# Talking-heads attention and squared-ReLU feed-forward: a planner that holds on-chip relayouts when a burst of loads begins

## The chip, the cores and the metric

The kernel runs on one core of one Trainium2 chip. The metric is the device time of one execution in microseconds (us), as the median of several runs. Besides that there is one profiled execution, from which all single durations are taken.

## The reference

Eight batches, twelve heads, 448 positions, head size 64; then a feed-forward block of 768 to 2048 to 768 on the attention's output of 3584 tokens.

```python
scores = scale * np.matmul(q, k.transpose(0, 1, 3, 2))
scores = np.einsum('bhij,hg->bgij', scores, w_pre)      # heads are mixed before the softmax
scores = scores - np.max(scores, axis=-1, keepdims=True)
attn = np.exp(scores)
attn = attn / (np.sum(attn, axis=-1, keepdims=True) + 1e-09)
attn = np.einsum('bhij,hg->bgij', attn, w_post)         # and once more after it
out = np.matmul(attn, v)
x = out.transpose(0, 2, 1, 3).reshape(B * S, H * D)
h = np.maximum(x @ w_in, 0.0)
result = h * h @ w_out
```

## The kernel before

**The work and its pieces.** A batch is cut into 45 *chunks* of up to ten query rows times twelve heads, 120 partitions. The head mixing is then a matmul over a chunk's 120 rows. The steps, with the lines of the profile:

- `score` (L681): scores of one head pair and one row block, evacuated by DVE (L487) or ACT (L489) into `snat`, where rows are positions. `b` is the batch, `r` the row block 0 to 3.
- `relayout` / `move` (L709): DMAs on SP's queue that gather a chunk's rows out of `snat` into `sch`, where rows are (position, head). There are two `snat` buffers, so a score block's evacuation overwrites the block before last and must see that block's relayouts landed.
- `chunk`: the mixing matmul (L807; in batch 0 partly L813, straight from the queries through weights prepared on DVE at L796), row minimum on DVE (L818, scores carry a minus sign), exponential with sum on ACT (L821), reciprocal on DVE (L827), the second mixing's weights times that on POOL (`wq`, L830), second mixing and transpose in one (L837), evacuation into `atb` (L487, L489).
- `av` (L882): times the values, evacuated into `xt`.
- `unit`: the feed-forward for 128 or 256 tokens: L941, ReLU on DVE (L955) or ACT (L959), square on POOL (`h`, L962), L980, evacuation into `osb`, and stores (L1004).
- `x_piece` (from batch 2 on): K and Q of the next batch, copied into `kn` and `qn` on POOL or DVE (L612), then transposed by DMA on SP's queue (L625, L631); `x_tail` (L596) does the same for the tail rows. In batches 0 and 1 PE transposes (L549, L577).
- Loads of q, k, v and the feed-forward weights are DMAs issued by POOL (L352, L358, L363, L1076, L1082). Those of the next batch come in a burst of eight, once a batch.
- Idle matmuls (L1191) stand where the plan has PE idle early in the kernel.
- At the start the mixing weights are made: `near_mix` (L467) on DVE, turned by one matmul (L1054), put by DVE (L1060).

**What sets the order.** A planner. Each step is an operation with one or several possible engines, a cost in ns, a priority, a latency `lat` after it and its dependencies. `Planner.run` plays all engines forward in its own time, each always taking its most urgent ready operation, and records the operations in that order. The recorded order is the program: each engine then works through its own list, and waits where the data is not there. The planner's times set the order and nothing else.

**Transfers in the planner.** Two modelled queues, `LOAD` (POOL's loads) and `DMA` (relayouts and stores). `moved(queue, rows, alone, shared, ...)` is a transfer of so many rows with a cost per row when the other queue is empty or not. A relayout is an SP operation followed by such a transfer; a load likewise from POOL; a store (`st_op`) likewise. If `DMA` is empty while loads run, a relayout first waits for the loads that are ahead (`ahead`, at most `FIFO` rows).

`AHEAD` is by how many chunks the relayout of a chunk is more urgent than its mixing; the scores' priority follows from it too.

Of the kernel before, what the change touches and what calls it, by code (L numbers as in the profile page):

```python
# [39 lines left out]
PIECE = NPAIR // 2  # L40
NE = 6
NSCH = 11
AHEAD = 7.0
FIFO = 50
IDLE_NS, IDLE_COLS, IDLE_FROM, IDLE_END, IDLE_LOW = 112, 256, 1300, 130000, 0.62
SPELL, PHASE, DROP, RISE = 3413, 1700, 0.4, 0.8
ROWS, COLS = 1, 2
TURN = 95
LATER = 2
NEAR_LAST = 2e6  # L50
OSTEP = 2
GS, ONE = [(0, 1, 2)], [(0,), (1,), (2,)]
# [26 lines left out]
NEAR_AT = 5  # L79
# [42 lines left out]
class Planner:  # L122
# [8 lines left out]
    def add(self, eng, ns, pri, fn, deps=(), lat=60, bank=None, frees=None, mode=0):  # L131
        op = Op(eng if isinstance(eng, dict) else {eng: ns}, lat, pri, fn, list(deps), bank, frees, mode)
        self.ops.append(op)
        return op
# [6 lines left out]
    def run(self):  # L141
        order, events, n = [], [], 0
# [21 lines left out]
        t, mode, clock = 0, 0, Clock()  # L164
        queues = {"LOAD": Queue(), "DMA": Queue()}

        def settle():
            nonlocal n
            a, z = queues["LOAD"], queues["DMA"]
            for x, y in ((a, z), (z, a)):  # L170
                if x.op is None:
                    continue
                x.left -= (t - x.at) * x.rate
                x.at = t
                rows, alone, shared = x.op.rows
                x.rate = 1.0 / (alone if y.op is None else shared + y.op.rows[2])
                x.turn += 1
                heapq.heappush(events, (t + max(x.left, 0.0) / x.rate, n, (x, x.turn)))
                n += 1

        while True:
            for eng, heap in ready.items():
                if eng in queues:
                    x = queues[eng]
                    y = queues["LOAD"]
                    if eng == "DMA" and x.op is None and heap and y.op is not None and x.last != t and x.wait < t:
                        ahead = max(0.0, y.left - (t - y.at) * y.rate) + sum(z[2].rows[0] for z in ready["LOAD"])
                        x.wait = t + int(min(ahead, FIFO) * y.op.rows[1])
                        heapq.heappush(events, (x.wait, n, None))
                        n += 1  # L190
                    if eng == "DMA" and x.wait > t:
                        continue
                    while x.op is None and heap:
                        op = heapq.heappop(heap)[2]
                        op.eng, op.at = eng, t
                        order.append((op, []))
                        if op.rows[0] == 0:
                            heapq.heappush(events, (t + op.lat, n, op))
                            n += 1
                            continue  # L200
                        x.op, x.left, x.at, x.rate = op, float(op.rows[0]), t, 0.0
                        settle()
                    continue
                if busy[eng] > t:
                    continue
                kept, short, first = [], False, None
                while heap:
                    item = heapq.heappop(heap)
                    op = item[2]
                    if op.eng is not None:  # L210
                        continue
                    wide = len(op.bank) > 1
                    if not fits(op) or (short and op.bank and op.bank[0][0] in HOLD):
                        short = short or wide
                        kept.append(item)
                        continue
                    if eng == "PE" and mode and op.mode != mode and first is None:
                        first = item
                        kept.append(item)
                        continue  # L220
                    if first is not None:
                        if op.mode != mode or op.pri > first[0] + STAY[mode]:
                            kept.append(item)
                            if op.pri > first[0] + STAY[mode]:
                                op, item = first[2], first
                                kept.remove(first)
                            else:
                                continue
                    args = []
                    break  # L230
                else:
                    item = None
                    if first is not None:
                        kept.remove(first)
                        item, op, args = first, first[2], []
                if item is None and eng == "PE" and free and IDLE_FROM <= t < IDLE_END and (
                    t < 9000 or clock.at(t) > 1 or clock.share(t - SPELL, t) < IDLE_LOW
                ):
                    op = Op({"PE": 0}, 0, 0, self.still, [], None, None, mode)
                    op.eng, op.ns, op.at = "PE", IDLE_NS * clock.at(t), t  # L240
                    clock.spells.append((t, t + op.ns))
                    order.append((op, [free[0], mode]))
                    busy[eng] = t + op.ns
                    heapq.heappush(events, (t + op.ns, n, None))
                    n += 1
                if item is not None:
                    for key in op.bank:
                        held[key] = free.pop(0)
                        room[key[0]] -= 1
                        room["mix"] -= key[0] != "f"  # L250
                        args.append(held[key])
                    if len(op.engs) > 1:
                        args.append(eng)
                    op.eng, op.ns, op.at = eng, op.engs[eng], t
                    if eng == "PE":
                        op.ns = (op.ns + TURN * (op.mode != mode)) * clock.at(t)
                        clock.spells.append((t, t + op.ns))
                        mode = op.mode
                    order.append((op, args))
                    busy[eng] = t + op.ns  # L260
                    heapq.heappush(events, (t + op.ns, n, None))
                    heapq.heappush(events, (t + op.ns + op.lat, n + 1, op))
                    n += 2
                for item in kept:
                    heapq.heappush(heap, item)
            if not events:
                break
            t = events[0][0]
            while events and events[0][0] == t:
                op = heapq.heappop(events)[2]  # L270
                if op is None:
                    continue
                if isinstance(op, tuple) and isinstance(op[0], Queue):
                    x, turn_ = op
                    if x.turn == turn_:
                        done = x.op
# [27 lines left out]
def kernel(  # L304
# [11 lines left out]
    nc = tc.nc  # L316
# [175 lines left out]
    pl = Planner()  # L492
    pl.banks, pl.most = banks, MOST
    add = pl.add
# [32 lines left out]
    h_op, sq_op, o_op, st_op = {}, {}, {}, {}  # L527
# [141 lines left out]
    def score(b, r, group):  # L669
# [13 lines left out]
        first = min(place_of(b, c) for c in range(C0[r], (C0 + [NCHUNK])[r + 1]) if not is_direct(b, c)) - b * NCHUNK  # L683
        pri = b * NCHUNK + first - AHEAD - 0.6 - (0.7 if r == 0 else 1.4) * (NPAIR - p)
        n = b * (NJ + 1) + r - 2
# [20 lines left out]
        return r, c - C0[r]  # L706

    def move(n, pri, ns, deps, outs, srcs, lat):
        op = add("SP", ns, pri, lambda: nc.sync.dma_start(out=outs, in_=srcs), deps, lat=680)  # L709
        rows, alone, shared = (12, 70, 38) if ns > 700 else (6, 70, 38)  # L710
        done = pl.moved("DMA", rows, alone, shared, 0, [op], 500)
        relay.setdefault(n, []).append(done)
        return done

# [209 lines left out]
    def unit(pair, ui):  # L924
        a, z = units_of(pair)[ui]
# [46 lines left out]
        for mt in range(w // 128):  # L972
            whole = not (z == W2B and mt == 1 and pair == B // 2 - 1)
            cuts = [0, 384, DMODEL] if whole else [0, 384, 640, DMODEL]
            for nt, (c0, c1) in enumerate(zip(cuts, cuts[1:])):
# [16 lines left out]
                si = ix_store[0]  # L992
# [6 lines left out]
                if nt == 1 or not whole:  # L999
                    done = []  # L1000
                    for rows, dst, o in pieces(pair, a + mt * 128, None if whole else (c0, c1)):
                        side_ = not whole and rows <= CI
                        def store(dst=dst, o=o, rows=rows, si=si, e0=0 if whole else c0, e1=DMODEL if whole else c1, eng=nc.scalar if side_ else nc.sync):
                            eng.dma_start(out=dst, in_=osb[si % 2][o:o + rows, e0:e1])  # L1004
                        done.append(add("ACT" if side_ else "SP", 510 if rows <= CI else 930, FILL, store, evs))
                    st_op[si] = pl.moved("DMA", 8, 140, 130, 0, done, 1500)
            if whole:
                ix_store[0] += 1

# [53 lines left out]
    backed_far.append(add("POOL", 420, FAR_AT, far_back, [picked]))  # L1063
    fetched = add("DVE", 900, NEAR_AT, pick_near, [walled, k_in[0, 2]])
    masked = add("DVE", 500, NEAR_AT, near_masks, [k_in[0, 2]])
    mixed = add("DVE", 500, NEAR_AT, near_mix, [fetched, masked])
    backed.append(add("POOL", 420, NEAR_AT, near_back, [fetched, masked]))
    w_ready = add(
        "DVE", 300, NEAR_AT, w_put, [add("PE", 200, NEAR_AT, keep(("m", "w"), w_turn), [mixed], lat=200, bank=("m", "w"))], frees=("m", "w"),
# [162 lines left out]
```

## Time and profile before

| | us |
|---|---|
| three runs | 578.25, 578.26, 579.37 |
| median | 578.26 |
| the profiled execution's own time | 577.99 |
| its span, first to last instruction | 576.2 |
| busy PE in it | 565.1 |
| busy DVE, ACT, POOL | 510.2, 445.9, 329.4 |
| mean granted clock of TensorE | 0.999 |

PE is the engine of the matmuls, DVE the vector engine, ACT the scalar engine, POOL the GpSimd engine and SP the engine that issues most DMAs; PEld is the weight load of PE. A line of the timeline or of a group tells engine, line of the kernel, operation, what it writes and reads, and how many; in brackets the engine's idle time before it and who ended that. A matmul's record is longer than its share of PE's time, since matmuls overlap: a run of L807 matmuls starts one each 0.19 us, though each record lasts 0.35 us.

### The profile page before, as it was taken

The page shows a single profiled execution, that of the slowest core. Times are in us where ns is not written, and L with a number is a line of the kernel's source. Part 1 is how long each engine was busy: PE and PEld are TensorE (multiplying, and loading weights), DVE is VectorE, ACT ScalarE, POOL GpSimd, SP SyncE. Part 2 cuts the span into 40 slices and gives each one's busy share as a digit, 9 for nine tenths or more (in the row PEclk, how much of TensorE's full clock was granted, in tenths as well). Part 3 has the DMA queues.
Part 4 walks back from the last instruction along what each step waited for, and adds up shares of the span by engine and source line. Part 5 has one row for each costly group of instructions (what it writes and reads, how often), then busy time and mean ns, then how long its engine had stood idle before and what let it go on. Part 6 is the DMA issues. An engine that isn't in the chain of part 4 may idle for free.

```text
span 576.2 us, 16829 instructions
## 1 busy us (share of the span) xinstructions
PE 565.1 (98%) x5830; PEld 407.5 (71%) x5830; DVE 510.2 (89%) x1124; ACT 445.9 (77%) x1185; POOL 329.4 (57%) x609
## 2 busy tenths in 40 slices
PE   8999999999999999999999999999999999999997
PEld 5668766786776767677667677777758676767784
DVE  7999998999999999989899988999799898989442
ACT  5798988878778887988888988888888888888100
POOL 8267445764575548646567357845767444735341
PEclk9999999999999999999999999999999999999999
DMA  9999849963898639963697638984497646322021
GB/s 135 211 182 224 158 116 208 163 151 87 132 202 156 159 100 184 173 151 111 137 181 148 164 104 144 188 152 139 109 205 158 147 121 117 124 81 75 1 56 55
DMA packets 131678, 80.79 MB, mean 140 GB/s; under 512 B 59286, under 2 KB 126600, under 8 KB 131592
## 3 DMA queue, kind: packets, MB, share of 16 engines
q1 hardware_dynamic: 84760, 56.88, 40.3%
q0 software_dynamic: 46784, 22.81, 30.8%
q8 instruction: 45, 0.74, 0.6%
q14 instruction: 41, 0.34, 0.2%
q10 hardware_dynamic: 48, 0.02, 0.0%
HBM read 45.61 MB, written 11.01 MB: 98 GB/s over the span
## 4 chain that ended last, share of the span: by engine, by line
PE 87%; DVE 6%; DMA 3%; ACT 2%; issue 1%; POOL 0%; DVEq 0%; ACTq 0%; POOLq 0%
PE bank L980 24%; PE bank L941 23%; PE bank L837 12%; PE bank L807 11%; PE bank L882 7%; PE bank L681 6%; DMA sch<-snat 3%; PE bank L813 2%; DVE mn L818 1%; DVE atb L487 1%; DVE snat L487 1%; PE bank L1191 1%; ACT es L821 1%; DVE qn L612 1%; ACT snat L489 0%
## 5 line engine op out<-in xcount | busy, mean ns | idle before, releaser
L821 ACT ACTIVATE es<-bank,mn 120x448 bf16<-120x448 f32 x360 | 228.5, 643 | 37.0 <-DVE mn L818 32.6
L818 DVE TENSOR_REDUCE mn<-bank 120x1 f32<-120x448 f32 x360 | 209.7, 611 | 1.2 <-PE bank L807 1.1
L830 POOL TENSOR_SCALAR wq<-wback,rc 120x120 bf16<-120x120 f32 (+1 forms) x346 | 123.0, 367 | 148.4 <-DVE rc L827 90.3
L980 PE MATMUL bank<-w,h 128*128 128x384 bf16 (+2 forms) x912 | 184.1, 323 | 0.0
L941 PE MATMUL bank<-xt,w 128*128 128x256 bf16 (+1 forms) x1632 | 164.7, 254 | 0.3 <-ACT hr L959 0.2
L962 POOL TENSOR_TENSOR h<-hr 128x512 bf16<-128x512 f32 x112 | 116.4, 1041 | 64.8 <-DVE hr L955 34.9
L941 PEld LDWEIGHTS <-w 128*128 128x128 bf16 x1632 | 136.1, 98 | 22.8 <-issue 2.4
L837 PEld LDWEIGHTS <-es 120*112 120x112 bf16 (+1 forms) x1440 | 110.9, 129 | 27.7 <-ACT es L821 3.7
L837 PE MATMUL bank<-wq,es 120*112 120x120 bf16 (+1 forms) x1440 | 120.8, 217 | 0.5 <-ACT es L821 0.2
L980 PEld LDWEIGHTS <-h 128*128 128x128 bf16 x912 | 83.7, 98 | 51.7 <-issue 5.2
L487 DVE CAST atb<-bank 112x480 bf16<-112x480 f32 (+3 forms) x184 | 112.9, 622 | 7.8 <-PE bank L837 4.9
L489 ACT CAST atb<-bank 112x480 bf16<-112x480 f32 (+3 forms) x199 | 103.8, 537 | 19.1 <-PE bank L837 18.3
L807 PE MATMUL bank<-sch,wmix 120*128 120x448 bf16 (+1 forms) x339 | 108.2, 354 | 2.6 <-DVE snat L487 2.0
L487 DVE CAST snat<-bank 128x448 bf16<-128x448 f32 x153 | 89.1, 612 | 4.8 <-PE bank L681 2.7
L489 ACT CAST snat<-bank 128x448 bf16<-128x448 f32 x165 | 81.8, 546 | 7.7 <-PE bank L681 7.2
L821 ACT ACTIVATION_READ_ACCUMULATOR es<-bank,mn 120x1 f32 x360 | 75.1, 209 | 0.0
L955 DVE TENSOR_SCALAR hr<-bank 128x512 f32<-128x512 f32 x75 | 51.6, 688 | 19.3 <-PE bank L941 16.9
L807 PEld LDWEIGHTS <-wmix 120*128 120x128 bf16 (+1 forms) x346 | 31.2, 97 | 23.7 <-issue 10.9
L882 PE MATMUL bank<-atb,vs 112*64 112x192 bf16 (+3 forms) x864 | 40.4, 250 | 0.1
L681 PE MATMUL bank<-kt,qz 64*128 64x448 bf16 x276 | 39.7, 354 | 0.5 <-DVE snat L487 0.2
L882 PEld LDWEIGHTS <-vs 112*64 112x64 bf16 x864 | 36.5, 110 | 3.9 <-issue 2.4
L487 DVE COPY osb<-bank 128x384 f32<-128x384 f32 (+2 forms) x42 | 22.8, 543 | 16.8 <-PE bank L980 16.2
(72 smaller groups left out, 316.7 us busy)
## 6 DMA issues: line engine op xcount, KB each, us to landing
sch<-snat SPq DMA_DIRECT2D x318, 105.0 KB
out_dram<-osb SPq DMA_DIRECT2D x22, 360.0 KB
vs<-in_v_dram POOLq DMA_DIRECT2D x16, 336.0 KB, 8.4
ks<-in_k_dram POOLq DMA_DIRECT2D x14, 336.0 KB, 8.2
qs<-in_q_dram POOLq DMA_DIRECT2D x14, 288.0 KB, 9.1
w<-in_moe_w_in_dram POOLq DMA_DIRECT2D x6, 512.0 KB, 13.5
w<-in_moe_w_out_dram POOLq DMA_DIRECT2D x4, 768.0 KB, 21.4
out_dram<-osb SPq DMA_DIRECT2D x8, 192.0 KB
```

The costliest lines, as they stand in the source:

```text
L487: nc.vector.tensor_copy(out=out_, in_=in_)
L489: nc.scalar.copy(out=out_, in_=in_)
L681: nc.tensor.matmul(slot[:, 0:S], lhsT=lhsT, rhs=kt[i][half, :, at_, :], start=True, stop=True)
L807: nc.tensor.matmul(slot[:, 0:S], lhsT=wm[0:rows, :], rhs=src[0:rows, :], start=True, stop=True,)
L818: nc.vector.tensor_reduce(out=mn[i][0:rows, :], in_=slots[mk][0:rows, 0:S], axis=AX.X, op=ALU.min)
L821: nc.scalar.activation(out=es[i][0:rows, 0:S], in_=slots[mk][0:rows, 0:S], func=ACT.Exp, scale=-1.0, bias=mn[i][0:rows, 0:1], accum_out=sm ...
L830: nc.gpsimd.tensor_scalar(out=wq[i][0:rows, :, 0:ns], in0=back[0:rows, :, 0:ns], scalar1=rc[i // 2][0:rows, i % 2:i % 2 + 1], scalar2=1.0, ...
L837: nc.tensor.matmul(slot[0:P_KEYS, jb * H * ns:(jb + 1) * H * ns], lhsT=es[i][0:rows, jb * P_KEYS:(jb + 1) * P_KEYS], rhs=wq[i][0:rows, :, ...
L882: nc.tensor.matmul(v_[64 * hh:64 * hh + 64, i, 0:x1 - x0], lhsT=vs[:, 2 * c2 + hh, jb, :], rhs=atb[half][:, jb, 2 * c2 + hh, x0:x1], start ...
L941: nc.tensor.matmul(slot[:, j * w:(j + 1) * w], lhsT=w1[c2][:, (f0 + j) * 128:(f0 + j + 1) * 128], rhs=xt[:, c2, a:z], start=(c2 == 0), sto ...
L962: nc.gpsimd.tensor_tensor(out=h2_[:, f0:f0 + nf, 0:w], in0=hr[gi % 2][:, :].rearrange("p (f c) -> p f c", f=nf), in1=hr[gi % 2][:, :].rear ...
L980: nc.tensor.matmul(slot[:, 0:c1 - c0], lhsT=h2_[:, ft, mt * 128:(mt + 1) * 128], rhs=w2[:, ft, c0:c1], start=(ft == 0), stop=(ft == FT - 1),)
```

## The change

Five edits, all in the planner's figures:

- a load that finds its queue idle for over 2.5 us (after the first 20 us) starts a *burst*: the `DMA` queue, if empty, takes nothing for 3.8 us; if a transfer is under way, that one gets the rows that make it 3.8 us longer;
- relayouts: the latency of SP's operation falls from 680 to 400 ns, that of the transfer from 500 to 350;
- stores: the cost of each of 8 rows rises from 140 to 170 ns alone and from 130 to 215 ns shared;
- the mixing weights (`near_mix`) get a latency of 600 ns, where the default of 60 stood;
- `AHEAD` falls from 7.0 to 6.9.

```diff
-AHEAD = 7.0
+AHEAD = 6.9
...
+ONSET, ONSET_IDLE, ONSET_FROM = 3800, 2500, 20000
...
                         x.op, x.left, x.at, x.rate = op, float(op.rows[0]), t, 0.0
+                        if eng == "LOAD" and t - max(x.last, 0) > ONSET_IDLE and t > ONSET_FROM:
+                            z = queues["DMA"]
+                            if z.op is None:
+                                z.wait = t + ONSET
+                                heapq.heappush(events, (z.wait, n, None))
+                                n += 1
+                            else:
+                                z.left += ONSET / (z.op.rows[2] + op.rows[2])
                         settle()
...
     def move(n, pri, ns, deps, outs, srcs, lat):
-        op = add("SP", ns, pri, lambda: nc.sync.dma_start(out=outs, in_=srcs), deps, lat=680)
+        op = add("SP", ns, pri, lambda: nc.sync.dma_start(out=outs, in_=srcs), deps, lat=400)
         rows, alone, shared = (12, 70, 38) if ns > 700 else (6, 70, 38)
-        done = pl.moved("DMA", rows, alone, shared, 0, [op], 500)
+        done = pl.moved("DMA", rows, alone, shared, 0, [op], 350)
...
-                    st_op[si] = pl.moved("DMA", 8, 140, 130, 0, done, 1500)
+                    st_op[si] = pl.moved("DMA", 8, 170, 215, 0, done, 1500)
...
-    mixed = add("DVE", 500, NEAR_AT, near_mix, [fetched, masked])
+    mixed = add("DVE", 500, NEAR_AT, near_mix, [fetched, masked], lat=600)
```

The instructions of the two programs are the same but for their order, the engine of some copies, evacuations and ReLUs, the banks that matmuls write to, and the number of idle matmuls (44 before, 38 after). The lines of the changed kernel stand nine higher from `run` on.

## The prediction

> **What bounds the kernel now.** I read the page first, then TensorE's busy time by stage, then who waited for whom on PE, then the timeline at the stages where PE lost time.
>
> ```profile
> PE 565.1 (98%) x5830; PEld 407.5 (71%) x5830; DVE 510.2 (89%) x1124; ACT 445.9 (77%) x1185; POOL 329.4 (57%) x609
> ...
> PE 87%; DVE 6%; DMA 3%; ACT 2%; issue 1%; POOL 0%; DVEq 0%; ACTq 0%; POOLq 0%
> ```
>
> PE is the bound: the change neither adds nor removes a needed matmul, so it can only win what PE loses in waiting. The stage table (stretch; its length, busy us of PE, and so on) says how much that is:
>
> ```profile
> 0.00:20.00 20.00, 17.10 (x165) 10.81 (x166) 16.62 (x55) 12.03 (x26) 13.50 (x25) 1.00 1.15 156
> 20.00:80.00 60.00, 58.77 (x756) 42.79 (x754) 57.59 (x143) 52.40 (x143) 32.55 (x62) 1.00 0.99 181
> 80.00:100.00 20.00, 19.07 (x202) 12.04 (x201) 17.76 (x41) 17.07 (x46) 11.11 (x22) 1.00 1.00 182
> 100.00:160.00 60.00, 60.00 (x631) 43.95 (x628) 57.56 (x125) 47.79 (x129) 36.70 (x68) 1.00 0.74 137
> 160.00:180.00 20.00, 18.87 (x171) 13.06 (x170) 19.68 (x39) 15.95 (x43) 14.48 (x26) 1.00 1.04 189
> ...
> 290.00:310.00 20.00, 19.27 (x179) 13.96 (x178) 19.76 (x41) 17.09 (x45) 13.94 (x25) 1.00 1.06 179
> 310.00:540.00 230.00, 229.71 (x2367) 168.40 (x2366) 208.06 (x448) 191.38 (x512) 131.34 (x248) 1.00 0.61 131
> ```
>
> Idle PE is 2.90 us at the start, 1.23 + 0.93 + 0 + 1.13 + 0 + 0.73 + 0.29 = 4.3 us from 20 to 540 us, and 3.9 us in the tail, where the last evacuation and store run and nothing is changed. So the middle can give 4.3 us, hardly more. Most of it is three places. The first, with the 1.27 us idle on DVE, is the one that the new model is about:
>
> ```profile
> 96.25 0.62 DVE L487 CAST snat<-bank 128x448 bf16<-128x448 f32 x1 [1.27 <-DMA out_dram<-osb]
> ...
> 96.92 0.35 PE L807 MATMUL bank<-sch,wmix 120*128 120x448 bf16 x1 [0.92 <-DVE snat L487]
> ```
>
> The label names a store, but the queue is SP's, and what must have landed are the relayouts that read the old snat. Taking a relayout's landing as the last update of its semaphore in the trace: one issued at 84.54 us landed at 88.88, the next, issued at 85.40, at 92.74, then 93.75, 94.92, 95.93. That gap of 3.86 us opens as the loads' packets start at 86.0 us; at four other bursts it is 2.95 to 3.6 us. Away from bursts a relayout lands a median 2.9 us after issue, and 6.7 at the ninth tenth; inside one, 7 to 8. So the 3.8 us of the new constant is in this trace.
>
> The other two places are no transfers: a copy of qn on DVE stands still while POOL runs two squares in a row, and everything behind it on DVE is late.
>
> ```profile
> 166.25 2.90 DVE L612 COPY qn<-qs 128x384 bf16<-128x384 bf16 x1
> ...
> 166.95 2.04 POOL L962 TENSOR_TENSOR h<-hr 128x512 bf16<-128x512 f32 x2
> ...
> 169.73 0.92 PE L807 MATMUL bank<-sch,wmix 120*128 120x448 bf16 x3 [1.11 <-DVE snat L487]
> ```
>
> The same copy takes 0.28 us elsewhere. At 297.00 us another takes 2.40 us against two squares that end at 299.24, and PE loses 0.43 and 0.17 us right after it.
>
> **The change part by part.** It changes the planner's figures alone, and the plan is the program's order: 85% of PE's 1,635 groups (idle matmuls apart) stand at another place in their queue, though only 21% by more than five places. I compare the two orders by leads: the PE work, in program order, between a transfer's issue or an evacuation and the matmul that needs it, at the trace's start-to-start times (190 ns an L807, 109 or 56 an L941, 162 an L980, 52 an L837).
>
> The hold at a burst (seven bursts after 20 us): the relayouts that the scores of batch 1, row block 3, must see landed (the wait of 96 us) are issued 5.5 us of PE work ahead before, and 12.2 us ahead after; in a burst they need 7 to 8. That wait goes: -0.92 us. What comes due next there is the batch's ordinary work, with leads of 10 us and more for all its relayouts. For the other bursts the same lead goes from 10.9, 9.2, 10.9, 8.1, 6.3, 11.4 to 8.9, 7.7, 8.4, 12.4, 10.0, 15.3: none under 7.7, two near the need. Bound: 0 to +1 us; I take +0.3.
>
> Latencies of relayouts (680 to 400 ns on SP, 500 to 350 on landing) and AHEAD 7.0 to 6.9 (0.1 chunk, 0.14 us at 510 us for 360 chunks): a mix may stand 0.43 us closer behind its relayout. Over 367 relayouts the median lead stays at 11.7 us and the tenth percentile goes from 8.6 to 8.9, but the shortest from 4.7 to 3.7. Those are the first four relayouts of batch 2 (leads 4.7 to 6.2 before, 3.7 to 5.1 after). Before, the first of them took 2.7 us from issue to landing, and its mix started 2.3 us after that; so 1 us less still fits: 0, with the price of a slow landing in the rival below.
>
> Stores (1.12 to 1.36 us of the modelled queue alone): they move a few places on SP; a 12x10x768 store now stands ahead of the last relayout, whose mix comes some 10 us later, and SP issues one in 0.83 us. Cost 0; if that cover were gone, 0.8.
>
> The mixing weights (60 to 600 ns): L1054 moves behind the first score pair and one set of transposes. Its wait goes, but not the time:
>
> ```profile
> 10.91 0.26 PE L1054 MATMUL bank<-wmix,perm 120*120 120x120 bf16 x1 [0.86 <-DVE wmix L467]
> ...
> 11.24 0.36 PE L681 MATMUL bank<-kt,qz 64*128 64x448 bf16 x2
> ```
>
> DVE's order is unchanged up to the second qz copy, which ends near 11.4, the first near 11.2; the scores that now stand first wait for that first copy, as before. The first far chunk stands 0.76 us of PE work earlier, but its operand comes from DVE: a snat copy (0.61), a qz copy (0.34), three L796 (0.33 each), another qz copy, an L796, the two L1060 (0.45) and an L796 from about 11.6 us on, with some waits for PE between, which ends near 15 us, and L813 started at 15.25. I take 0, bounds -0.5 to +0.5. Six idle matmuls fewer (0.11 us each of stream): they only fill waits, 0.
>
> What the new order moves by the way: five of 19 copies of kn and qn go from DVE to POOL (0.51 or 0.61 us each, +2.8 us on an engine busy 57%), seven relus from ACT to DVE and six osb copies back; with the trace's means by form DVE gets 2.3 us less, ACT 0.4 less. The gain is in which copies stay: of the 14 none stands beside two squares in a row, while before two did, and these cost 1.11 and 0.43 + 0.17 us. -1.71 us. Next late there: a DVE copy beside one square waits at most its 1.04 us, which the work between covers; if not, 14 copies could give back up to 1 us in a place or two. The five on POOL cost nothing while wq has slack (POOL sat idle 148 us before wq); at worst 2.8.
>
> Short leads by count: groups of matmuls whose lead is less than the operations in between take, without any queueing, number 35 before and 53 after; the next class, up to 300 ns, falls from 103 to 73. In the trace the first class lost 95 ns each and the second 47: +1.7 - 1.4 = +0.3 us.
>
> Sum: -0.92 - 1.71 + 0.3 + 0.3 = -2.0 us against the profiled execution, 577.99 us (span 576.2, and 1.8 around it): 576.0. The median of the three runs is 578.26, 0.27 above; on that scale 576.2, and I say 576.1. The forecast's own range is 574.0 to 577.1: the ends are -1.7 for what else of the 4.3 and the head goes, and +1.0 for the two near leads.
>
> One rule speaks against the change. In this trace no relayout lands for 3.86 us, and then one every 1.0 us. The Trainium skill (DMA: Bandwidth & Descriptors, "Issuing engines are not separate DMA queues") says that transfers from all issuing engines run on the same 16 engines and interleave with each other: that would be slower relayouts, not a hold. The trace disagrees for the first 3 to 4 us of a burst.
>
> **The rivals.** *Slower: relayouts too near their use.* Place: the first relayouts of batches 2 and 3, leads 3.7 to 5.1 and 5.9 to 6.8 us. For: the model now promises them 0.43 us sooner, PE takes its queue in order, so one late mix stops all, and transposes (4.3 to 5.6 us to landing in the median) and stores share SP's queue just ahead. Against: before, with 4.7 us, 2.3 us were left. It decides from a landing time of 3.7 us on. At 6.7 us in batch 2 and a burst's 7.9 in batch 3, it costs 3.0 + 2.0 us: 576.1 + 5.0 = 581.1. Chance 0.27.
>
> *No change to speak of: the waits only move.* The three places were accidents of one order, and the new order has 18 more of the shortest leads, around 48, 62 and 192 us. If they lose as much as one such place (0.9 us) at two spots, 576.1 + 1.8 = 577.9. Chance 0.18.
>
> *The hold is not one.* If bursts only slow relayouts, by interleaving, the 12.2 us lead was not needed and the 96 us wait comes back in another burst: 576.1 + 0.9 = 577.0, still faster by 0.2%. The landings speak against it. Chance 0.05.
>
> **How the numbers follow.** Forecast 0.50. A measurement of this kernel tells about 0.2% (1.2 us) from no change. Faster is 0.50 + 0.05 = 0.55, the same 0.18, slower 0.27. The range, 573.5 to 580.8, reaches below the forecast's end by 0.5 for unknown gains in the head, and up to just under the slower rival's price; what it leaves out is the upper part of that rival and a little below, together 0.2.
>
> **What would show it.** Right: idle PE near zero at the batch 1 burst (80 to 100 us), and in the stages after 160 and 290 us; no L612 copy on DVE above 1.3 us; L681 taking L1054's wait at 11 us. Wrong: PE waits at L807 for sch at the start of batch 2 (near 140 us) or 3; a POOL that is late with wq; new waits of over 1 us on DVE's evacuations in the bursts near 150 or 215 us; PE busy unchanged with a shorter or longer span would mean that the loss is in matmul pace and not in waits.

## The result, and the profile after

The changed kernel takes 583.47 us (median of five runs, 581.71 to 584.13), the kernel before 578.38 in the same measurement. The ratio of the means is 1.0077, with a 95% interval of 1.0057 to 1.0096: a loss of 0.8%, clear of the noise. Forecast were 576.1 us, with a range of 573.5 to 580.8. The profiled execution took 584.13 us (span 582.3), the longest of the five, against 577.99 (span 576.2): 6.1 us to explain.

The page of the changed kernel, engines, clock and chain:

```profile
PE 568.3 (98%) x5824; PEld 408.4 (70%) x5824; DVE 507.1 (87%) x1121; ACT 447.2 (77%) x1183; POOL 332.9 (57%) x614
...
PEclk8899999999999999999999999999999999999999
...
PE 87%; DVE 6%; ACT 2%; DMA 1%; issue 1%; POOL 1%; SPq 0%; DVEq 0%; POOLq 0%; ACTq 0%
```

PE is the bound as before. New is the 8 at the left of PEclk: the granted clock was 0.5 from 11.3 us on for 6.8 us. The table by stage, in the stretches shown of before (length, then busy us of PE, PEld, DVE, ACT, POOL, clock, DMA share, GB/s):

```profile
0.00:20.00 20.00, 16.29 (x149) 10.35 (x150) 14.39 (x47) 9.81 (x20) 13.21 (x24) 0.83 1.15 157
20.00:80.00 60.00, 57.77 (x734) 41.29 (x733) 56.19 (x138) 52.30 (x139) 32.44 (x58) 1.00 0.99 179
80.00:100.00 20.00, 19.64 (x199) 12.47 (x198) 18.62 (x42) 18.37 (x50) 11.85 (x24) 1.00 0.70 129
100.00:160.00 60.00, 58.94 (x621) 42.17 (x618) 54.69 (x119) 48.31 (x127) 34.98 (x66) 1.00 0.73 137
160.00:180.00 20.00, 19.70 (x190) 14.86 (x189) 19.36 (x42) 18.01 (x50) 16.94 (x30) 1.00 1.09 202
180.00:290.00 110.00, 107.94 (x1111) 78.24 (x1109) 101.24 (x223) 89.99 (x240) 64.71 (x125) 1.00 0.74 143
290.00:310.00 20.00, 20.00 (x173) 13.01 (x172) 19.61 (x43) 17.02 (x47) 13.16 (x25) 1.00 1.10 190
310.00:540.00 230.00, 229.68 (x2325) 167.01 (x2323) 207.55 (x448) 189.35 (x508) 132.64 (x250) 1.00 0.63 134
```

The three stretches with the named waits of before have lost them: idle PE at 80 to 100 us fell from 0.93 to 0.36, at 160 to 180 from 1.13 to 0.30, at 290 to 310 from 0.73 to 0. Three others paid: the first 80 us (3.71 + 2.23 idle, before 2.90 + 1.23, and the clock), 100 to 160 (1.06, before 0) and 180 to 290 (2.06, before 0).

To sum this without the stretches' edges I use *PE's lag*: at each matmul group, the time of its start less the sum of the start-to-start times of all useful matmuls ahead of it. It grows only where PE waits, idles along or runs slowly. Read at the same amount of useful PE work, its growth compares two orders stage by stage:

| useful PE work, us | before | after | difference |
|---|---|---|---|
| 0 to 38 (head) | 13.59 | 17.77 | +4.18 |
| 38 to 60 | 5.27 | 4.88 | -0.39 |
| 60 to 80 (burst in batch 1) | 2.13 | 0.68 | -1.45 |
| 110 to 120 (start of batch 2) | 0.39 | 1.99 | +1.60 |
| 140 to 160 | 2.22 | 1.17 | -1.05 |
| 170 to 180 (start of batch 3) | 0.52 | 2.84 | +2.32 |
| 260 to 290 | 2.19 | 1.05 | -1.14 |
| 400 to the end | 2.74 | 3.93 | +1.19 |
| all others | 8.23 | 9.02 | +0.79 |

So the predicted gains are there, 3.6 us of them. The losses are the head, the starts of batches 2 and 3, and a smear over the end that no single wait explains. One profile is one execution: a second profile of the same order, below, differs from this one by 1.3 us in the head and by 2.7 at the start of batch 3.

The head in the timeline after (L690 is the score, L558 PE's transposes, L496 and L498 the evacuations on DVE and ACT). PE waits for the first copy of qz, twice as long as it had waited for L1054, and then the clock is halved:

```profile
9.70 0.53 PE L558 MATMUL bank<-ident,qs 128*64 128x128 bf16 x12 [0.98 <-DMA qs<-in_q_dram]
11.90 0.55 PE L690 MATMUL bank<-kt,qz 64*128 64x448 bf16 x2 [1.67 <-DVE qz L496]
12.38 0.85 PE L558 MATMUL bank<-ident,qs 128*64 128x128 bf16 x12
```

The start of batch 3, SP's queue, PE and one of the two engines that copy (DVE):

```profile
197.31 2.33 SPq L634 DMA_TRANSPOSE kt<-kn  x1
199.75 1.65 SPq L640 DMA_TRANSPOSE qz<-qn  x1
201.49 1.70 SPq L718 DMA_DIRECT2D sch<-snat  x2
...
203.97 0.35 PE L690 MATMUL bank<-kt,zt 128*128 128x448 bf16 x1
...
205.10 1.16 DVE L496 CAST snat<-bank 128x448 bf16<-128x448 f32 x2 [2.62 <-DMA out_dram<-osb]
205.78 0.54 PE L690 MATMUL bank<-kt,zt 128*128 128x448 bf16 x2 [1.45 <-DVE snat L496]
```

The same matmuls in the kernel before, without a wait:

```profile
199.09 0.73 PE L681 MATMUL bank<-kt,zt 128*128 128x448 bf16 x3
```

A score block of batch 3 (row block 1) is to be copied into `snat` over a block of batch 2. The copy must see the last two relayouts of batch 2 landed; they stand on SP behind two transposes, issued at 201.49, and land at 203.9 and 204.7 us (the label again names a store). DVE and ACT wait (2.62 and 2.29 us idle there), the banks stay full, PE stops. Against the plan's own times SP slips from 2.9 us late at 157 us to 8.0 at 202, PE only from 3.1 to 3.6. Of SP's 5.1 us, 2.3 are the five transposes between 178 and 201 us: they hold SP for 10.5 us where the plan has 8.2. In the kernel before SP slips by 2.7 us over that stage (153 to 197 us), and PE, held up by a copy of qn, by 1.5. My reading is that there PE's own waits gave SP its time; no run tests this alone.

### The profile page after: what moved, and what is told of

It reads as the page before. It is cut to its first block, busy times and chain, and to the rows that moved or that the text cites. A ratio compares the mean times of both kernels' runs of the same rounds, so it can differ in the third digit from the quotient of the medians.

```text
span 582.3 us, 16782 instructions
## 1 busy us (share of the span) xinstructions
PE 568.3 (98%) x5824; PEld 408.4 (70%) x5824; DVE 507.1 (87%) x1121; ACT 447.2 (77%) x1183; POOL 332.9 (57%) x614
## 4 chain that ended last, share of the span: by engine, by line
PE 87%; DVE 6%; ACT 2%; DMA 1%; issue 1%; POOL 1%; SPq 0%; DVEq 0%; POOLq 0%; ACTq 0%
PE bank L989 25%; PE bank L950 24%; PE bank L846 13%; PE bank L816 11%; PE bank L891 7%; PE bank L690 6%; DVE mn L827 2%; PE bank L822 2%; DVE atb L496 1%; ACT es L830 1%; DMA out_dram<-osb 1%; DVE hr L964 1%; PE bank L1200 1%; DMA qz<-qn 1%; POOL wq L839 1%
## 5 line engine op out<-in xcount | busy, mean ns | idle before, releaser
L496 DVE CAST atb<-bank 112x480 bf16<-112x480 f32 (+2 forms) x189 | 114.0, 611 | 8.4 <-PE bank L846 6.2
L498 ACT CAST atb<-bank 112x480 bf16<-112x480 f32 (+2 forms) x194 | 102.9, 546 | 15.1 <-PE bank L846 13.6
L816 PE MATMUL bank<-sch,wmix 120*128 120x448 bf16 (+1 forms) x339 | 106.8, 353 | 0.2
L496 DVE CAST snat<-bank 128x448 bf16<-128x448 f32 x154 | 89.5, 612 | 6.1 <-DMA out_dram<-osb 2.8
L498 ACT CAST snat<-bank 128x448 bf16<-128x448 f32 x164 | 81.4, 543 | 9.8 <-PE bank L690 6.1
L964 DVE TENSOR_SCALAR hr<-bank 128x512 f32<-128x512 f32 x82 | 56.4, 688 | 16.4 <-PE bank L950 13.5
L690 PE MATMUL bank<-kt,qz 64*128 64x448 bf16 x276 | 40.1, 360 | 2.2 <-DVE qz L496 1.7
L496 DVE COPY osb<-bank 128x384 f32<-128x384 f32 (+2 forms) x36 | 19.5, 542 | 19.2 <-PE bank L989 18.4
```

The source lines that it names most:

```text
L496: nc.vector.tensor_copy(out=out_, in_=in_)
L498: nc.scalar.copy(out=out_, in_=in_)
L690: nc.tensor.matmul(slot[:, 0:S], lhsT=lhsT, rhs=kt[i][half, :, at_, :], start=True, stop=True)
L816: nc.tensor.matmul(slot[:, 0:S], lhsT=wm[0:rows, :], rhs=src[0:rows, :], start=True, stop=True,)
```

## The experiments

Every ratio is that of the mean times, to the kernel before measured beside it on the same chip. Times of different groups of runs are compared by these ratios, as the kernel before itself had medians from 577.81 to 578.91 us.

### The changed kernel again, and three ways to split it

> The changed kernel once more, unaltered. In its first profile TensorE's granted clock stands at 0.5 for 6.8 us from 11.3 us on, and PE is 2.7 us later than before by the first far chunk and 4.4 us later by 35 us. Theory 'clock': the loss in the head is the half clock, so a run with full clock is about 3.4 us faster than the profiled 584.1, some 580.7. Theory 'waits': the wait for DVE's qz copy (1.67 us) and what follows is there at any clock, and the time stays at 582 to 584 with the clock at 1.0.

Measured: 584.05 us, ratio 1.0098 (1.0080 to 1.0115). Theory 'clock' does not hold for the whole: among the nine executions of this order two had a granted clock of 1.0, and they took 583.60 and 581.71 us, not 580.7. In the second profile the half clock in the head lasted 3.4 us instead of 6.8, the head lost 1.3 us less than in the first, and the start of batch 3 lost more, a lag of +5.5 us instead of 2.8:

```profile
205.31 0.54 PE L690 MATMUL bank<-kt,zt 128*128 128x448 bf16 x2 [3.08 <-DVE snat L496]
```

What the head gave back, batch 3 took: PE resumes there at 205.31 us, against 205.78 in the first profile, when SP's relayouts have landed.

An edit with no content, on the kernel before (80% of PE's groups stand elsewhere):

```diff
-        x = max_op[n] = add("DVE", 540, n + 0.3, f_max, [m, exp_op.get(n - NE)], lat=110)
+        x = max_op[n] = add("DVE", 541, n + 0.3, f_max, [m, exp_op.get(n - NE)], lat=110)
```

> The kernel before, with one planner cost changed that means nothing: the row minimum on DVE costs 541 ns in the plan, not 540. No edit of the change is in it, yet 80% of PE's groups stand at another place. Theory 'places' (the edits cost at nameable places: the mixing weights in the head, relayouts behind transposes on SP's queue): this order has none of the edits, 578.4 plus or minus 1.2. Theory 'draw' (any fresh order of this plan loses what a lucky order had): slower by 1 to 5 us, 579.5 to 583.5.

Measured: 578.58 us, 1.0003 (0.9990 to 1.0016), as theory 'places' has it. A new order as such need not lose. Between 60 and 80 us of work its lag grew by 1.1 us where the kernel before has 2.1, without any hold.

The kernel before with the later mixing weights alone (`near_mix`, `lat=600`):

> The kernel before with the 600 ns latency of the mixing weights alone. Theory 'places': the head's loss comes with it, 2.7 to 4.4 us by 35 us of the span, so 581 to 583; L1054 stands behind the first scores and PE waits for DVE's qz copy instead. Theory 'draw': the head is as before within 0.5 us, and the total is wherever this order falls, 577 to 583.

Measured: 581.48 us, 1.0063 (1.0040 to 1.0086), again as theory 'places' has it. Its lag at 38 us of work is 16.4 us, 2.9 over the kernel before and 2.1 over the order without content.

The changed kernel without that edit:

> The changed kernel without the 600 ns latency of the mixing weights; the four other edits stay. Theory 'places': the head is as before (lag at 35 us within 0.5 us of before's), and what remains is the later loss of about 1.6 us: 579.5 to 580.5. Theory 'draw': no such order, 577 to 584, with losses at places of its own.

Measured: 584.91 us, 1.0116 (1.0097 to 1.0135), above both ranges: theory 'places' falls here. The other four edits lose as well, at other places; the losses of single edits don't add up.

### The starts of batches 3 and 2

SP's list alone is edited, after the planner has run; at batch 3 the last two relayouts go ahead of both transposes:

```diff
-TURN = 95
+TURN, SWAP = 95, [(3, (0, 1))]
...
-        for op, args in pl.run():
+        plan = pl.run()
+        for b, late in SWAP:
+            last = moves[b * NCHUNK - 1]
+            at = next(i for i, x in enumerate(plan) if x[0] is last)
+            held = [x for x in plan[:at] if any(x[0] is turns[b, 1][i] for i in late)]
+            plan = [x for x in plan[:at + 1] if x not in held] + held + plan[at + 1:]
+        for op, args in plan:
```

> The changed kernel with one edit in SP's list: at the start of batch 3 the two relayouts that come last of batch 2 are issued ahead of the two DMA transposes, and nothing else moves on any engine. Theory A (place on SP's list): the copy of batch 3's first score block (L496, out of its bank into snat) waits for these two relayouts, which stand behind 2.33 + 1.65 us of transposes; issued some 4 us earlier they land near 200 us instead of 204.7, so the waits at 204 to 207 us (1.45 us of PE on snat, 2.4 us of lag in all) go, and the time is 581.1 us, 580.3 to 582.0. Rival B (the transposes are the next to be late): they land 1.8 us later, 204.4 and 206.9 us, and the second half of the batch's score blocks waits for them instead; then 583.0 to 583.9. Rival C (the transfers themselves are late, not their issue): the landings stay at 204 us and nothing changes, 583.5.

Measured: 581.96 us, 1.0081 (1.0051 to 1.0110); the changed kernel had 1.0077 and 1.0098. The bare time lies inside theory A's range, but the kernel before stood at 577.81 us beside it, and by the ratio nothing was gained. The timeline of this kernel, SP and PE:

```profile
196.19 1.66 SPq L718 DMA_DIRECT2D sch<-snat  x2
197.94 2.08 SPq L634 DMA_TRANSPOSE kt<-kn  x1
200.13 1.30 SPq L640 DMA_TRANSPOSE qz<-qn  x1
...
203.98 0.74 PE L690 MATMUL bank<-kt,zt 128*128 128x448 bf16 x3 [1.80 <-DMA kt<-kn]
```

The wait for snat is gone, and in its place PE waits 1.80 us for the transpose, which landed at 203.9 us. That is rival B: whichever of the two stands last on SP is late.

At batch 2 as well (`SWAP = [(2, (0,)), (3, (0, 1))]`):

> As the run before, and at the start of batch 2 too the last relayout of batch 1 is issued ahead of the DMA transpose of K in front of it (2.33 us). Theory A: the waits at 137.9 us (ACT 1.26, DVE 0.96, PE 1.00 us; 1.5 us of lag) go as well: 579.6 us, 578.8 to 581.0, which leaves about 1.2 us over the kernel before, in the head. Rival B: 583 to 584. Rival C: 583.5.

Measured: 582.61 us, 1.0073 (1.0051 to 1.0095): theory A falls. The lag grows by 0.6 us at the start of batch 2 (after: 2.0), but the run before, without this edit, shows the same 0.6: nothing is shown for batch 2. A new wait stands at batch 4; SP, POOL and PE there:

```profile
238.79 3.76 SPq L634 DMA_TRANSPOSE kt<-kn  x1
...
238.89 0.83 POOL L372 DMA_DIRECT2D ks<-in_k_dram  x1
...
252.08 0.54 PE L690 MATMUL bank<-kt,zt 128*128 128x448 bf16 x2 [2.34 <-DMA kt<-kn]
```

The transpose landed at 251.9, 13.2 us after issue, and a load of ks, issued 0.1 us after it, at 251.7. The first profile of the changed kernel has the same pair, issued 0.1 us apart and landing 0.2 us apart after 10 us, though there PE did not wait for it. In the kernel before that load had been issued 4.9 us ahead of the transpose, which landed in 7.7. The planner gives a transpose a fixed latency; neither the hold nor the loads reach it.

The changed kernel without the two transposes (`turn_k` and `turn_q` of batch 3, second half, do nothing):

> The changed kernel without the two DMA transposes of the second half of batch 3's heads (the K and the Q of heads 6 to 11 of that batch are left out, so these heads use what the batch before left in kt and qz). SP's list is 4.0 us shorter just ahead of the two relayouts that came late. Theory A (SP's list is what is late at the start of batch 3: the two relayouts or the two transposes, whichever stand last, keep PE waiting): with neither behind the other the wait at 204 us goes, the lag step there falls from 2.3 to 0.4 us, and the time is 581.3 us, 580.3 to 582.3. Rival H (PE is late there for another reason, and the wait only changes its name): 583 to 584.

Measured: 582.44 us, 1.0053 (1.0034 to 1.0071). The stage table of the changed kernel, and then of this one:

```profile
198.00:215.00 17.00, 15.09 (x175) 10.56 (x173) 13.86 (x30) 11.72 (x31) 6.93 (x12) 1.00 0.59 134
```

```profile
198.00:215.00 17.00, 17.00 (x182) 11.51 (x180) 16.91 (x37) 13.19 (x35) 8.44 (x17) 1.00 0.40 102
240.00:280.00 40.00, 37.68 (x353) 27.12 (x352) 34.23 (x74) 29.96 (x81) 21.07 (x42) 0.96 0.73 124
```

With 4 us less on SP, PE is busy for all of the 17 us, as theory A has it: SP's list is what was late at batch 3. The time, just above A's range and below H's, shows little of it: of the 1.9 us gained, most went again at 252 us in the wait for batch 4's transpose (2.32 us) that the run before showed.

### The clock in the head

Twelve idle matmuls ahead of the first score pair:

```diff
+    pl.still, warm = stand, [0] * 12
...
         for op, args in pl.run():
+            while warm and op.mode == ROWS:
+                stand(args[0], warm.pop())
```

> The changed kernel with one edit: twelve idle matmuls (128x128 by 256 columns, some 0.1 us each) stand on PE ahead of the first score pair, where PE waits 1.2 to 2.0 us for the copy of qz; the planned order is otherwise the same. Theory F (a part of the head's loss is the clock: after this wait the granted clock was 0.5 for 6.8 us in the first profile of this order and for 3.4 us in the second): no half-clock stretch in the first 20 us, and the time falls from some 583.7 to 582.0, range 581.0 to 583.0. Rival G (the head is paced by DVE, and the low clock falls into time that PE would wait anyway): 583.3 to 584.2.

Measured: 585.07 us, 1.0102 (1.0082 to 1.0123). The timeline of PE:

```profile
9.68 1.48 PE L1200 MATMUL bank<-still 128*128 128x256 bf16 x12
11.96 0.36 PE L690 MATMUL bank<-kt,qz 64*128 64x448 bf16 x2 [0.80 <-DVE qz L496]
...
203.18 0.91 PE L690 MATMUL bank<-kt,zt 128*128 128x448 bf16 x2 [2.40 <-DVE snat L496]
```

The half clock is gone from the head, and the time is not better; it lies above both ranges. L690 starts when DVE has copied, with or without a warm PE. But the head itself did gain: by the same sums of lag it lost about 2.0 us against the kernel before, where the two profiles of the changed kernel lost 4.2 and 2.9. So rival G is wrong about the head, and the gain was lost again behind it: at batch 3 the wait is 2.40 us instead of 1.45, and against the first profile some 2 us more go after 200 us of useful work.

The kernel before knows the low clock too. Of its 62 executions beside these runs, the seven with a mean granted clock of 0.993 or 0.994 took 580.25 us in the mean, the 23 with 1.0 took 578.15.

### Single edits, and other orders

The hold alone, and the relayouts' latencies alone, on the kernel before:

> The kernel before with the hold of 3.8 us at a burst's start as its only edit. Theory A (the gains come from the hold, the losses from the head's edit and from relayouts that stand late on SP's list): the hold alone brings the 2.6 us of the prediction's first two terms where the plan keeps the last relayouts of a batch early, as it does at both starts here: 576.3 us, 575.0 to 578.0. Rival D (any model that shifts the transfers against the transposes on SP loses, the hold too): 579.5 to 582.

Measured: 581.76 us, 1.0072 (1.0050 to 1.0094): rival D, and theory A falls.

> The kernel before with the shorter latencies of a single relayout (400 + 350 ns instead of 680 + 500) as its only edit. Theory A: the shortest modelled lead of the first score block of a batch over the last relayout's issue falls to 2.7 us (batch 3), where the kernel before has 3.7 (batch 2), and the measured time from issue to landing is 2.27 us at its shortest: waits of about 1 us at one or two batch starts, 579.5 us, 578.5 to 581.5. Rival D: the change loses at other places as well, 581 to 584. Rival E (the order alone decides, the latencies are better): 577 to 578.5.

Measured: 581.50 us, 1.0067 (1.0044 to 1.0090), where theory A and rival D meet. But neither kernel has a wait for snat or kt at the start of batch 3 (lag +0.44 and +0.29 there). So theory A named a place of one order, not the cost of an edit.

Two more edits with no content on the kernel before (`TURN` 95 to 94; a score pair 190 to 191):

> The kernel before with the planner's cost of a change of matmul mode at 94 ns instead of 95, an edit with no content that gives another order from the first batch on. Theory I (the order of the kernel before is an unusually good one of many, and any edit that makes another order loses some 0.6%, whatever it says): 580 to 583. Rival J (orders lose by what the edits say): 577.5 to 579.3, as the other edit without content did.

> The kernel before with the planner's cost of a score pair at 191 ns instead of 190, again an edit with no content and another order from batch 1 on. Theory I: 580 to 583. Rival J: 577.5 to 579.3.

Measured: 581.66 us, 1.0042 (1.0020 to 1.0064), and 580.54 us, 1.0030 (1.0012 to 1.0048). Both lie in the lower half of theory I's range and outside rival J's, where the first such edit (1.0003) lay. So the old order was a good draw, by some 0.25%. Three such edits on the changed kernel:

> The changed kernel with the planner's cost of a row maximum at 541 ns instead of 540: no content, another order (83% of PE's groups stand elsewhere, from the 67th on). Theory I (the five edits say nothing harmful; the changed kernel is one draw among the orders that such a model gives, as the kernel before is another): like the orders of the kernel before with edits of no content, 578.5 to 581. Theory K (the edits themselves cost, whatever order comes of them): 582 to 585.

> The changed kernel with the planner's cost of a change of matmul mode at 94 ns instead of 95. Theory I: 578.5 to 581. Theory K: 582 to 585.

> The changed kernel with the planner's cost of a score pair at 191 ns instead of 190. Theory I: 578.5 to 581. Theory K: 582 to 585.

Measured: 587.93 us, 1.0146 (1.0120 to 1.0172), 581.27 us, 1.0041 (1.0028 to 1.0055), and 585.53 us, 1.0111 (1.0084 to 1.0138): one just above theory I's range, two above theory K's. The mean of the three edits on the kernel before is 1.0025; that of the changed kernel (1.0098) and its three is 1.0099. By these means the changed figures cost 0.7% or 4.3 us, and one order stands up to 0.6% from the mean of its kind. That is a likely cost and no sure one, for the orders are few and the two kinds meet (1.0042 and 1.0041). But all seven kernels here with only some of the five edits lie above every order without content of the kernel before, at 1.0063 to 1.0173. How an order falls is seen in part in the first of the three: DVE's list has a copy of kn whose load comes late, all behind it wait, and PE with them. Its timeline:

```profile
233.66 0.29 DVE L621 COPY kn<-ks 112x512 bf16<-112x512 bf16 x1 [4.46 <-DMA ks<-in_k_dram]
...
234.64 0.60 PE L950 MATMUL bank<-xt,w 128*128 128x256 bf16 x4 [3.04 <-DVE atb L496]
```

The changed kernel without the hold:

> The changed kernel without the hold (the lines in the planner's run are left out), the other four edits kept. By the prediction the hold brought the larger part of the 2.6 us of gains: without it 585 to 586. Theory I: an order like any other, 578.5 to 583. Theory L (the hold is what packs the transfers so late ahead of batches 3 and 4): 579 to 581.

Measured: 588.71 us, 1.0173 (1.0156 to 1.0190), the slowest of all and above every theory. Its timeline, first in the burst whose packets begin at 153.7 us, then some 10 us later:

```profile
168.72 0.53 ACT L498 CAST snat<-bank 128x448 bf16<-128x448 f32 x1 [3.50 <-DMA sch<-snat]
...
169.31 0.42 PE L846 MATMUL bank<-wq,es 120*112 120x120 bf16 x4 [2.29 <-ACT snat L498]
...
177.07 2.90 DVE L621 COPY qn<-qs 128x384 bf16<-128x384 bf16 x1
...
177.77 2.04 POOL L971 TENSOR_TENSOR h<-hr 128x512 bf16<-128x512 f32 x2
...
181.08 0.35 PE L816 MATMUL bank<-schl,wmix 96*128 96x448 bf16 x1 [2.13 <-DVE snat L496]
```

The relayouts issued at 157.6 to 159.7 us took 8.1 to 8.9 us to land. The wait at 169 us is the one that the hold is made against, and with the hold it isn't there. The wait at 181 us is the other kind, a copy of qn beside two squares, which has nothing to do with transfers. Between 140 and 170 us of work the lag grows by 7.9 us without the hold and by 1.2 with it, but that is both waits together, in one order of each kind.

The changed kernel with the old relayout latencies, and with neither these nor the later mixing weights:

> The changed kernel with the latencies of a single relayout as before (680 + 500 ns), the other four edits kept. Theory M (the shorter latencies are the edit that costs: with them the plan puts users of relayouts 0.4 us nearer, so that every lateness of SP's list reaches PE): 578.5 to 580.5. Rival N (the order matters more than this edit): anywhere from 581 to 588, as the orders of the changed model did.

> The kernel before with the hold, the stores' new cost and the lead of 6.9, and neither the shorter relayout latencies nor the later mixing weights. Theory M, with the head's loss undone as well: 576.5 to 578.5, the best of all. Rival N: 580 to 586.

Measured: 582.98 us, 1.0071 (1.0053 to 1.0090), and 585.38 us, 1.0106 (1.0087 to 1.0124). Theory M falls: taking out the edit that I held for the costly one leaves the time within the scatter of the orders. No kernel here was faster than the kernel before.

## Why the prediction was wrong

- **PE is the bound, and only waits can change:** right, 98% busy in both.
- **The hold, -0.92:** the wait at 96 us went (lag -1.45). But an order without a hold lost it too, so it was an accident of the old order, and no measure of the hold. What the hold is worth stays open: the one order without it is 0.75% slower than the changed kernel, which is hardly more than one order's scatter and holds a qn wait besides, and the hold alone on the kernel before lost 0.7%.
- **The qn copies, -1.71:** came, -1.1 twice. The longest L621 copy on DVE is 0.96 us, where before two took 2.90 and 2.40. But this came with the draw of the order: the first order without content lost both as well, and of the kernels with most of the changed figures two have such a copy again (2.90 us without the hold, 2.47 with the hold and the stores' cost).
- **Near leads and short leads, +0.3 and +0.3, and the shortest relayout leads, 0:** this step failed, by 3.9 us in the first profile (1.6 + 2.3). The start of batch 3 lost in both profiles of this order and with the idle matmuls, and least in the first; the 1.6 at batch 2 did not come again in the runs with SP's list changed (growth of 0.6 there, 0.39 before). The step compared the leads of mixings over their relayouts and took each issue to come when the list says. The waiter was the score block's copy into `snat`, over the *last* relayouts of the batch before. In the plan the first such block of batch 3 stands 6.1 us behind their issue before and 3.7 after, and SP then slipped 4.6 us more than PE. The slower rival named batches 2 and 3, and transposes and stores on SP's queue, rightly; it had the mixings as the waiters, and its 581.1 us were still too few.
- **The mixing weights, 0:** failed, too. The bounds were 0.5 either way; the head lost 4.2 us in the first profile and 2.9 in the second. The runs show three parts. First, the copy of qz that the score pair waits for began at 11.50 us instead of 10.83. That is not the edit's doing: it began at 11.58 or 11.59 in three kernels without the edit (the first order without content, the hold alone, the latencies alone), and at 10.74 and 10.94 in the two with SP's list changed, which have it. These 0.7 us differ from execution to execution. Second, the clock, for which the step had no term: with a late copy and 6.8, 3.4 and 0 us of half clock the head lost 4.2, 2.9 and about 2.0 us, some 1 us for each 3.4. Third, the new order: with an early copy and the full clock (the run with both starts changed) about 1.4 us are left. Where these arise is not shown; DVE did 14.39 us of work in the first 20 us instead of 16.62, and it is 98% busy for the 30 us after.
- **"The waits only move":** given 0.18 and two spots of 0.9 us; it was the larger part of the truth. With PE's own wait at 169 us gone, PE reached the next batch's start ahead of SP, and shortening SP's list there moved the wait to batch 4 in two runs.
- **Size of the draw:** left out. Edits of no content move this kernel by 0 to 0.4%, as much as the whole forecast gain of 0.4%.
- **The forecast's own range:** its lower end is added wrongly, as 576.1 - 1.7 is 574.4 and not 574.0. Nothing hangs on it.

Open: which edits carry the 0.7%, how much of it is the draw of orders, and what makes the 1.2 us after 400 us of work. The wait at batch 3 is explained for this order alone.

## What to carry over

When a planner's figure changes, the whole order is drawn anew: measure a few edits without content first, since that scatter (here up to 0.6% around the mean) is what a forecast gain must exceed. Take several profiles of one order, too: the head here differed by 1.3 us between two of them, by the clock. Ahead of pricing a removed wait, set each engine's real times against its planned ones: the list that slips most (here SP's, by 4.6 us against PE) is the one to take the wait over when PE no longer waits elsewhere. A cost model that is mended at one place and not at its neighbours (relayouts held, transposes not) may pack the rest into times that do not hold; the batch 4 transpose suggests this, and no run separates it.

## What was not expected of the hardware

- **The clock drops after idle of less than 3.4 us.** After waits of PE of 2.32, 2.34, 2.40 and 3.08 us (batch 4 in two runs, batch 3 in two) the granted clock was 0.5 for 3.41 us; after one of 3.04 us, at 234.6 us in the run whose DVE waited for ks, it stayed at 1, and after 1.80 us too. In the head of the changed kernel, with waits of 0.98 and 1.67 us, it was 0.5 for 6.83 us. So the length of one wait does not decide alone. What fits is the idle time in a fixed window. In each of the 20 profiles all changes of the clock lie whole multiples of 3.41 us apart, so I cut the time between the first rise and the tail into such windows. Of the windows at full clock, all eleven with 1.88 us or more of idle PE were followed by half clock; of five with 1.67 to 1.80 us two were; below that, only one was (1.02 us, ahead of 40.8 us in the run without two transposes). The wait of 3.04 us lay across two windows, with 1.33 and 1.75 us in them. The Trainium skill (TensorE: Matmul & The Clock Gate, "Part 1: The HAM clock gate") puts the idle needed at one window of about 3.4 us: the length of the low stretches agrees, at one or two times 3.41 us, the idle does not.
- **A transpose occupies SP's queue for 1.2 to 5.4 us** over the 20 profiles, where the plan has 1.4 to 2.3, and takes 2.7 to 13.2 us to land.
- **A copy on DVE beside two squares on POOL takes 2.4 to 2.9 us** (2.90 and 2.40 us in the kernel before, 2.90 without the hold, 2.47 with the hold and the stores' cost), where a copy of qn on DVE has a median of 0.28 us in the changed kernel.
